# Row 1's overlap by transfers, the second dilated tile later, and the dilated v of rows 3 and 4 behind their transposes

## The chip, the cores and the metric

The kernel runs on one core of a Trainium2 chip, as one launch. The metric is device time in microseconds (us). Six runs of the kernel before gave 304.42 to 307.5, with a median of 305.58.

## The reference, cut to what matters

An attention over 8 batch rows, 8 heads, 576 tokens and 64 features feeds a two-layer network with a squared ReLU. Heads 0 to 3 see a sliding window of the last 32 tokens; heads 4 to 7 see every fourth of the last 128.

```python
B, H, S, D = 8, 8, 576, 64
rel = pos[:, None] - pos[None, :]
mask_plain = (rel >= 0) & (rel < 32)
mask_dil = (rel >= 0) & (rel < 128) & (rel % 4 == 0)
scores = where(mask of the head, q @ k.T / sqrt(D), -1e9)
attn = softmax(scores) @ v                    # per row and head
x = attn.transpose(0, 2, 1, 3).reshape(4608, 512)
h = x @ w_in                                  # 512 -> 2048
out = (maximum(h, 0) ** 2) @ w_out            # 2048 -> 512
```

## The kernel before, in words

**Two streams of work.** The attention goes by batch row (row 0 to row 7, 576 tokens each). The network goes by chunks of 512 tokens (chunk 0 to chunk 8). While row b's attention is computed, chunk b-1 of the network fills TensorE in between. The order of all instructions is written out by hand: each engine takes its instructions in the order in which the program records them, and waits for what it needs.

**Steps.** The network of a chunk is a generator (`moe_gen`), and `pump(n)` records n of its steps. In the first layer (`mm1_gen`) a step is two matmuls of a 128x512 tile `ph` (L305); two steps finish a tile, after which ScalarE takes the ReLU (`rt`, L328) and VectorE (DVE) the square (`g`, L329). So 32 steps make the first layer's 16 tiles. From chunk 2 on, the second layer (`mm2_strassen_gen`) is seven half-size products (L382) in place of eight; for that DVE forms sums of halves of g: `gs` (L338, L339), once after tile 11 and once, the last sums, after tile 15. TensorE reads them in the product named `pa<-wt,gs`, beginning with step 39; its fifth matmul is the first that needs the last sums. DVE then does a difference in g (L413) and one in gs (L425).

**The attention of a row.** `attn_scores` records four score groups, two sliding (`ps`, L588) and two dilated (`pz`, L613), each with a pump behind it. ScalarE takes the exponentials (`AT`, L572), DVE multiplies by the masks (`maskp`, `maskd`, L575). `attn_values` then records three sliding values tiles (`pav`, L643), and four dilated ones (`paw`, L659, for t = 0, 1 and a = 0, 1). DVE normalizes each (a reciprocal, L626, and a product into `xs` or `xd`, L631). The tiles pav and paw share two buffers in PSUM, so that each waits until the normalization of the tile two before is done. From row 4 on, `attn_values_by_dma` does the same, with the transposes of the result left to DMA.

**v and its overlap.** v is loaded in fp32 by SyncE's (SP's) DMA queue into `sv` (sliding) and `sd` (dilated), and GpSimd (POOL) casts it to fp16: `cast_sliding_v` makes three casts into `vp` (L169), `cast_dilated_v` four into `vd` (L177). Each sliding block of 96 queries needs 32 tokens of the block before it, and the second dilated tile (t = 1) needs 64 of the first. These are copied within vp and vd. `halo_sliding` and `halo_dilated` do it on ScalarE (L184: three copies a row, L189: two); `halo_sliding_by_dma` and `halo_dilated_by_dma` do it by one SP transfer each (L201, L204). Rows 0, 1 and 2 use ScalarE, rows 3 to 7 the transfers (from row 5 on, vp's copy is on DVE, L196).

**q and k of the next row.** POOL's DMA queue loads the sliding ones to `ns` (L112) and copies the dilated ones as fp16 to DRAM (`dd`, L214). DVE reorders ns into `nr` (`by_token`, L120), SP stores that (`dp`, L224), and SP transposes dp and dd into `QKTp` and `QKTd` (L232, L236). `turn` is the nr copy and the dp store. Before POOL loads the row after, it touches the last transposed tile (`seen`, L242), and so waits until that has landed.

**Where the next row's turn stands.** In rows 2 and 3 it is `turn_and_load`; row 2 records it behind the third pav, row 3 behind its second dilated score group. It records nr, dp, the loads of sv and sd, the four transposes, and all seven casts. From row 4 on, nr and dp stand behind the second (row 4) or third pav (rows 5 to 7), sd's load behind the transposes, and the dilated casts at the head of the next row, behind POOL's ns and dd.

The sums and the copy that the steps of the text follow:

```python
def sum_of_g(g, f0, f1):                      # DVE, L338 and L339
    k = slice(f0 - HF, f1 - HF)
    nc.vector.tensor_add(gs[0][:, k], g[:, k, HTOK:], g[:, f0:f1, HTOK:])
    nc.vector.tensor_sub(gs[1][:, k], gs[0][:, k], g[:, k, 0:HTOK])
```

Of the kernel before, what the change touches and what calls it, by code (L numbers as in the profile page):

```python
# [17 lines left out]
def kernel(  # L18
# [9 lines left out]
    nc = tc.nc  # L28
# [105 lines left out]
    def load_dilated_v(b, eng):  # L134
        vv = v[b, HH:H].rearrange("h (i c) d -> i h (c d)", c=DIL)
        for t in range(2):
            eng.dma_start(out=sd[P - QD[t] : P, t, :, :], in_=vv[Q0D[t] : Q0D[t] + QD[t]])
# [13 lines left out]
    def load_w_out(gs):  # L151
        for g in gs:
            nc.gpsimd.dma_start(
                out=wo[g],
                in_=moe_w_out[4 * g * P : 4 * (g + 1) * P, :].rearrange(
                    "(fl s) m -> fl (s m)", s=4
                ),
            )
# [8 lines left out]
    def cast_sliding_v(b, ms=range(0, NB, 2)):  # L167
        for m in ms:
            nc.gpsimd.tensor_copy(  # L169
                vp[b % 2][:, m : m + 2, :, 0:D], sv[:, :, m : m + 2, :].rearrange("p h m d -> p m h d")  # L170
            )

    def cast_dilated_v(b):
        for t in range(2):
            p0 = 64 * t
            for c in range(0, DIL, 2):
                nc.gpsimd.tensor_copy(  # L177
                    vd[b % 2][p0:P, t, c : c + 2, :, 0:D],
                    sd[p0:P, t, :, D * c : D * (c + 2)].rearrange("p h (c d) -> p c h d", d=D),
                )  # L180

    def halo_sliding(b, mp):
        m0, m1 = max(1, 2 * mp), 2 * mp + 2
        nc.scalar.copy(  # L184
            vp[b % 2][0:PADP, m0:m1, :, 0:D], vp[b % 2][P - PADP : P, m0 - 1 : m1 - 1, :, 0:D]
        )
# [13 lines left out]
    def halo_sliding_by_dma(b):  # L200
        nc.sync.dma_start(out=vp[b % 2][0:PADP, 1:NB], in_=vp[b % 2][P - PADP : P, 0 : NB - 1])  # L201

    def halo_dilated_by_dma(b):
        nc.sync.dma_start(out=vd[b % 2][0:64, 1], in_=vd[b % 2][64:P, 0])  # L204

    def cast_v(b):
        cast_sliding_v(b)
        cast_dilated_v(b)


    def keep_dilated_qk(b):
        d = dpool.tile([2, HH * CL, DIL * D], FP16, name=f"dd{b}", tag="dd")
        for i, src in ((1, k), (0, q)):
            nc.gpsimd.dma_start(  # L214
                out=d[i].rearrange("(r i) x -> r (i x)", i=4),
                in_=src[b, HH:H].rearrange("h (r i) d -> (h r) (i d)", i=16),
                max_dma_last_dim=4096,
            )
        return d
# [301 lines left out]
    def pump(n):  # L521
        for _ in range(n):
            while pending:
                try:
                    next(pending[0])
                    break
                except StopIteration:
                    pending.pop(0)
# [52 lines left out]
    def s_sliding(b, hp, between=None):  # L581
        tiles = [pa(f"ps{b}_{hp}_{half}") for half in range(2)]
        for half, ps in enumerate(tiles):
            for m3 in range(3):
                m = 3 * half + m3
                for e in range(2):
                    r = slice(D * e, D * (e + 1))
                    nc.tensor.matmul(  # L588
                        ps[:, e, QB * m3 : QB * (m3 + 1)],
                        QKTp[b % 2][r, 1, hp, QB * m : QB * m + P],  # L590
                        QKTp[b % 2][r, 0, hp, PADP + QB * m : PADP + QB * (m + 1)],
                        start=True,
                        stop=True,
                    )
        for half, ps in enumerate(tiles):
            exps(2 * hp + half, ps)
            if not between:
                masked(2 * hp + half, maskp)
        if between:
            between()  # L600
            for half in range(2):
                masked(2 * hp + half, maskp)
# [30 lines left out]
    def x_tiles(b):  # L633
        x = xp.tile([QB, 2, NB, 2, D], FP16, name=f"xs{b}", tag="xs")
        return x, [xp.tile([QD[t], DIL, HH, D], FP16, name=f"xd{b}_{t}", tag=f"xd{t}") for t in range(2)]
# [77 lines left out]
    def attn_scores(b, gap, less=0, hooks={}):  # L713
        for hp in range(2):
            s_sliding(b, hp)
            if hp in hooks:
                hooks[hp]()
            pump(gap)
        for g in range(2):
            s_dilated(b, g)  # L720
            if 2 + g in hooks:
                hooks[2 + g]()
            if g and b < 3:
                halo_sliding(b, 0)
            pump(gap - less)

    def attn_values(b, gap, wide=False, then=None):
        xs = x_tiles(b)
        for mp in range(3):
            av_sliding(b, mp, xs)  # L730
            if b < 3:
                if mp < 2:
                    halo_sliding(b, mp + 1)
                else:
                    halo_dilated(b, 0)
            if then and b == 2 and mp == 2:
                then()
            pump(gap)
        x_sliding(b, 0, xs, wide)
        if b < 3:  # L740
            halo_dilated(b, 2)
        pump(gap)
        av_dilated(b, 0, 0, xs)
        if then and b == 1:
            then()
        pump(gap)
        x_sliding(b, 1, xs, wide)
        pump(gap)
        av_dilated(b, 0, 1, xs)
        pump(gap)  # L750
        for a in range(2):
            av_dilated(b, 1, a, xs)
            pump(gap)
        x_dilated(b, 0, xs, wide)
        pump(gap)
        x_dilated(b, 1, xs, wide)

    def attn_values_by_dma(b, then):
        xs = x_tiles(b)
        for mp in range(3):  # L760
            av_sliding(b, mp, xs)
            if mp == (2 if b > 4 else 1):
                then[0]()
            pump(3)
        x_sliding_by_dma(b, xs)
        ys = []
        for t in range(2):
            for a in range(2):
                av_dilated(b, t, a, xs)
                pump(4 + 2 * (a > t))  # L770
            ys.append(x_dilated_by_dma(b, t, xs))
            then[1 + t](ys[t])
        pump(6)
        x_from(b, 0, ys[0])
        pump(7)
        x_from(b, 1, ys[1])
# [34 lines left out]
    nc.gpsimd.tensor_copy(sd[64:P, :, :, 0], wi[2][64:P, :, 0:2].rearrange("p d f -> p f d"))  # L811
    load_v(1)
    cast_sliding_v(1)
    load_w_out((3,))
    ns = load_sliding_qk(2)
    cast_dilated_v(1)
    dd = keep_dilated_qk(2)
    for mp in (1, 2):
        av_sliding(0, mp, xs)
# [42 lines left out]
    for b in range(2, 4):  # L862
        pending.append(moe_gen(b - 1))
        nxt = b + 1
        after_transposes(b)
        ns = load_sliding_qk(nxt)
        if b == 2:
            cast_v(b)
        dd = keep_dilated_qk(nxt)
        if b == 3:  # L870
            halo_sliding_by_dma(b)
            halo_dilated_by_dma(b)

        def turn_and_load():
            dp = turn(nxt, ns)
            load_sliding_v(nxt)
            load_dilated_v(nxt, nc.sync)
            transpose_sliding(nxt, dp)
            transpose_dilated(nxt, dd)
            cast_v(nxt)  # L880

        pump(22 if b == 2 else 12)
        attn_scores(b, 4, 0, {3: turn_and_load} if b == 3 else {})
        attn_values(b, b, False, turn_and_load)
        pump(1000)

    for b in range(4, B):
        pending.append(moe_gen(b - 1))
        nxt = b + 1
        if nxt < B:  # L890
            after_transposes(b)
            ns = load_sliding_qk(nxt)
            dd = keep_dilated_qk(nxt)
        if b > 4:
            cast_dilated_v(b)
        else:
            halo_sliding_by_dma(b)
        halo_dilated_by_dma(b)
        dps = []

        def copied():
            if nxt < B:
                dps.append(turn(nxt, ns))

        def first(y):
            if nxt < B:
                load_sliding_v(nxt)

        def second(y):
            if nxt < B:  # L910
                transpose_sliding(nxt, dps[0])
                transpose_dilated(nxt, dd)
                load_dilated_v(nxt, nc.sync)
                nc.gpsimd.tensor_copy(seen, y[:, 0, 0, 0:1])
                cast_sliding_v(nxt)
                at_end.append(lambda: halo_sliding_at_end(nxt))

        pump(3)
        attn_scores(b, 3)
        attn_values_by_dma(b, (copied, first, second))  # L920
        pump(1000)
    pending.append(moe_gen(B - 1))
# [32 lines left out]
```

## Time and profile before

| | us |
|---|---|
| median of six runs (lowest, highest) | 305.58 (304.42, 307.5) |
| profiled execution, its own time | 304.42 |
| its span, first to last instruction | 302.3 |
| busy: TensorE, DVE, ScalarE, POOL | 286.3, 209.7, 173.1, 62.0 |
| first ph matmul of chunk 2 (beside row 3) | 93.75 |
| of chunks 3, 4, 5, 6 (beside rows 4 to 7) | 125.38, 155.16, 185.95, 216.25 |

How to read it. PE is TensorE, PEld its weight loads, ACT ScalarE, and SPq SyncE's DMA queue. A row of the timeline has its start and duration in us, engine, line, operation, output<-inputs, shape and count; in brackets stands the idle time of the engine before it and what ended that. Operations on one engine overlap at their ends, so a g product of 0.42 recurs every 0.33 when they stand back to back, and two of them make 0.75. A row of the windows view has the window, its length, the busy time of PE, PEld, DVE, ACT and POOL with the number of their instructions, the granted clock, the DMA share and GB/s. A row of the waits has who waited for whom, the total in us, the times, and the longest.

### The profile page before, as it was taken

The page shows a single profiled execution, that of the slowest core. Times are in us where ns is not written, and L with a number is a line of the kernel's source. Part 1 is how long each engine was busy: PE and PEld are TensorE (multiplying, and loading weights), DVE is VectorE, ACT ScalarE, POOL GpSimd, SP SyncE. Part 2 cuts the span into 40 slices and gives each one's busy share as a digit, 9 for nine tenths or more (in the row PEclk, how much of TensorE's full clock was granted, in tenths as well). Part 3 has the DMA queues.
Part 4 walks back from the last instruction along what each step waited for, and adds up shares of the span by engine and source line. Part 5 has one row for each costly group of instructions (what it writes and reads, how often), then busy time and mean ns, then how long its engine had stood idle before and what let it go on. Part 6 is the DMA issues. An engine that isn't in the chain of part 4 may idle for free.

```text
span 302.3 us, 6890 instructions
## 1 busy us (share of the span) xinstructions
PE 286.3 (95%) x2760; PEld 192.0 (64%) x2760; DVE 209.7 (69%) x437; ACT 173.1 (57%) x293; POOL 62.0 (21%) x112
## 2 busy tenths in 40 slices
PE   1888998999999999999999999999999999999994
PEld 1454554555555468756889977568756975785583
DVE  7784448758852798489859984998499835734652
ACT  1856648568745953495358535953595356426620
POOL 4481009002605303320027002700230000000000
PEclk9999999999999999999999999999999999999999
DMA  6999997899599999996799999989983230003004
GB/s 113 195 198 214 206 182 133 184 211 229 128 212 183 240 205 179 247 201 124 129 182 256 191 133 191 265 179 164 179 230 41 41 139 0 2 4 136 3 0 139
DMA packets 77471, 46.77 MB, mean 155 GB/s; under 512 B 58432, under 2 KB 69184, under 8 KB 77440
## 3 DMA queue, kind: packets, MB, share of 16 engines
q1 hardware_dynamic: 68688, 32.71, 51.9%
q0 software_dynamic: 8752, 13.63, 26.4%
q8 instruction: 21, 0.34, 0.5%
q14 instruction: 10, 0.08, 0.1%
HBM read 36.70 MB, written 16.52 MB: 176 GB/s over the span
## 4 chain that ended last, share of the span: by engine, by line
PE 76%; DVE 7%; DMA 6%; ACT 4%; POOL 3%; issue 2%; DVEq 0%; POOLq 0%
PE ph L305 32%; PE pa L382 15%; PE po L450 9%; PE pb L382 8%; DMA vd<-vd 4%; PE pc L382 3%; DMA nd<-in_q_dram 2%; PE paw L659 2%; DVE g L329 2%; DVE xd L631 2%; PE ps L588 1%; ACT AT L572 1%; PE pav L643 1%; POOL ns L112 1%; DVE gs L338 1%
## 5 line engine op out<-in xcount | busy, mean ns | idle before, releaser
L305 PE MATMUL ph<-xT,wi 128*128 128x512 f16 (+1 forms) x640 | 134.2, 359 | 0.7 <-ACT xT L696 0.7
L328 ACT ACTIVATE rt<-ph 128x512 f16<-128x512 f32 x144 | 86.3, 609 | 44.5 <-PE ph L305 42.3
L305 PEld LDWEIGHTS <-wi 128*128 128x128 f16 x640 | 68.2, 114 | 45.8 <-issue 0.6
L329 DVE TENSOR_TENSOR g<-rt 128x512 f16<-128x512 f16 x144 | 63.1, 450 | 37.4 <-ACT rt L328 36.3
L382 PEld LDWEIGHTS <-g 128*128 128x128 f16 x448 | 43.3, 98 | 6.3 <-DVE g L329 0.2
L382 PEld LDWEIGHTS <-gs 128*128 128x128 f16 x336 | 32.0, 98 | 5.2 <-DVE gs L339 1.7
L450 PE MATMUL po<-wo,g 128*128 128x512 f16 x128 | 33.1, 379 | 0.0
L382 PE MATMUL pa<-wt,gs 128*128 128x256 f16 x224 | 27.6, 273 | 0.8 <-DVE gs L339 0.8
L409 DVE TENSOR_TENSOR ov<-pb,ov 128x512 f32<-128x512 f32 x14 | 9.7, 691 | 26.0 <-ACT ov L398 13.0
L382 PE MATMUL pb<-wt,g 128*128 128x256 f16 x224 | 27.1, 273 | 0.0
L398 ACT COPY ov<-pa 128x512 f32<-128x512 f32 x14 | 8.2, 585 | 31.0 <-PE pa L382 31.0
L169 POOL CAST vp<-sv 128x512 f16<-128x512 f32 x24 | 14.2, 626 | 53.1 <-DMA sv<-in_v_dram 49.2
L177 POOL CAST vd<-sd 128x512 f16<-128x512 f32 (+1 forms) x32 | 21.8, 708 | 10.9 <-DMA sd<-in_v_dram 8.1
L631 DVE TENSOR_TENSOR xd<-paw,rcp_d 80x512 f16<-80x512 f32 (+1 forms) x32 | 21.9, 684 | 1.1
L572 ACT ACTIVATE AT<-pz 128x576 f16<-128x576 f32 x32 | 19.8, 695 | 1.1 <-PE pz L613 1.1
L572 ACT ACTIVATE AT<-ps 128x576 f16<-128x576 f32 x32 | 19.2, 658 | 1.3 <-PE ps L588 0.8
L575 DVE TENSOR_TENSOR AT<-AT,maskd 128x576 f16<-128x576 f16 x32 | 17.6, 573 | 2.3 <-ACT AT L572 1.1
L575 DVE TENSOR_TENSOR AT<-AT,maskp 128x576 f16<-128x576 f16 x32 | 15.2, 484 | 4.8 <-ACT AT L572 3.0
L631 DVE TENSOR_TENSOR xs<-pav,rcp_p 96x512 f16<-96x512 f32 x24 | 16.5, 687 | 0.8
L398 ACT COPY ou<-pa 128x512 f32<-128x512 f32 x14 | 8.2, 585 | 13.9 <-PE pa L382 13.7
L450 PEld LDWEIGHTS <-g 128*128 128x128 f16 x128 | 10.4, 97 | 8.3
L659 PEld LDWEIGHTS <-AT 128*128 128x128 f16 x256 | 11.9, 98 | 5.6 <-PE paw L659 1.3
(81 smaller groups left out, 273.3 us busy)
## 6 DMA issues: line engine op xcount, KB each, us to landing
sv<-in_v_dram SPq DMA_DIRECT2D x14, 288.0 KB, 5.4
dp<-nr SPq DMA_DIRECT2D x12, 288.0 KB, 4.1
out_dram<-ou SPq DMA_DIRECT2D x6, 512.0 KB, 4.3
out_dram<-ov SPq DMA_DIRECT2D x6, 512.0 KB, 5.0
sd<-in_v_dram SPq DMA_DIRECT2D x8, 320.0 KB, 6.3
ns<-in_k_dram POOLq DMA_DIRECT2D x8, 288.0 KB, 6.7
ns<-in_q_dram POOLq DMA_DIRECT2D x8, 288.0 KB, 7.7
sd<-in_v_dram SPq DMA_DIRECT2D x8, 256.0 KB, 6.2
```

Of the source, the lines that this page charges most:

```text
L169: nc.gpsimd.tensor_copy(vp[b % 2][:, m : m + 2, :, 0:D], sv[:, :, m : m + 2, :].rearrange("p h m d -> p m h d"))
L177: nc.gpsimd.tensor_copy(vd[b % 2][p0:P, t, c : c + 2, :, 0:D], sd[p0:P, t, :, D * c : D * (c + 2)].rearrange("p h (c d) -> p c h d", d=D),)
L305: nc.tensor.matmul(ph[:, t0:t1], wi4[ffc // 4][:, dmk, :, ffc % 4], xT[:, dmk, x0 : x0 + t1 - t0], start=(dmk == 0 and t0 == 0), stop=(dmk ...
L328: nc.scalar.activation(rt, ph[:], ACTF.Relu)
L329: nc.vector.tensor_mul(g[:, ffc, :], rt, rt)
L382: nc.tensor.matmul(banks[bank][:, t], a(k, t), b(k), start=(new and t == 0 and k == 0), stop=(k == HF - 1), skip_group_check=True,)
L398: nc.scalar.copy(ot, banks[A])
L450: nc.tensor.matmul(po, g[:, ffc, t * P : (t + 1) * P], wo[ffc // 4][:, ffc % 4, :], start=(ffc == 0), stop=(ffc == NFF - 1),)
L572: nc.scalar.activation(AT[:, u, 0:UW], ps[:, :, 0 : UW // 2], ACTF.Exp, scale=scale)
L575: nc.vector.tensor_mul(AT[:, u, 0:UW], AT[:, u, 0:UW], mask)
L631: nc.vector.tensor_tensor(out=x, in0=pv, in1=rb, op=ALU.mult)
L659: nc.tensor.matmul(pav[:, e, h * (D + 2) : h * (D + 2) + D + 1], AT[:, 4 + h, off : off + P], vd[b % 2][:, t, 2 * a + e, h, 0 : D + 1], st ...
```

## The change

- **Row 1** takes the overlap of vp and vd by two SP transfers, recorded right behind the casts of each, in place of five ScalarE copies.
- **Rows 2 and 3** (`turn_and_load`): the load of sd stands behind the four transposes, and only the sliding casts remain there. The dilated casts of rows 3 and 4 move to the head of these rows, behind POOL's ns and dd and ahead of the vd transfer.
- **Row 3** records its scores after 9 steps and not 12, and its turn (nr and dp of row 4) behind the second pav in place of the second dilated score group.
- **Rows 4 to 7**: the second dilated tile (t = 0, a = 1) follows 7 steps behind the first in place of 4; 3 steps follow it in place of 6.

```diff
@@ attn_scores
-            if g and b < 3:
+            if g and b == 2:
                 halo_sliding(b, 0)
@@ attn_values
-            if b < 3:
+            if b == 2:
                 if mp < 2:
                     halo_sliding(b, mp + 1)
                 else:
                     halo_dilated(b, 0)
-            if then and b == 2 and mp == 2:
+            if then and b > 1 and mp == 4 - b:
                 then()
             pump(gap)
         x_sliding(b, 0, xs, wide)
-        if b < 3:
+        if b == 2:
             halo_dilated(b, 2)
@@ attn_values_by_dma
                 av_dilated(b, t, a, xs)
-                pump(4 + 2 * (a > t))
+                pump((7, 3)[a] if t == 0 else 4)
@@ before row 1
     cast_sliding_v(1)
+    halo_sliding_by_dma(1)
     load_w_out((3,))
     ns = load_sliding_qk(2)
     cast_dilated_v(1)
+    halo_dilated_by_dma(1)
     dd = keep_dilated_qk(2)
@@ rows 2 and 3
         dd = keep_dilated_qk(nxt)
         if b == 3:
+            cast_dilated_v(b)
             halo_sliding_by_dma(b)
             halo_dilated_by_dma(b)
 
         def turn_and_load():
             dp = turn(nxt, ns)
             load_sliding_v(nxt)
-            load_dilated_v(nxt, nc.sync)
             transpose_sliding(nxt, dp)
             transpose_dilated(nxt, dd)
-            cast_v(nxt)
-
-        pump(22 if b == 2 else 12)
-        attn_scores(b, 4, 0, {3: turn_and_load} if b == 3 else {})
+            load_dilated_v(nxt, nc.sync)
+            cast_sliding_v(nxt)
+
+        pump(22 if b == 2 else 9)
+        attn_scores(b, 4)
         attn_values(b, b, False, turn_and_load)
@@ rows 4 to 7
-        if b > 4:
-            cast_dilated_v(b)
-        else:
+        cast_dilated_v(b)
+        if b == 4:
             halo_sliding_by_dma(b)
         halo_dilated_by_dma(b)
```

## The prediction

> **What bounds the kernel now.** The page first: TensorE is busy nearly all of the span, at a granted clock of 0.9 or more in every slice. Only its gaps can be saved, so I looked next at TensorE's waits.
>
> ```profile
> PE 286.3 (95%) x2760; PEld 192.0 (64%) x2760; DVE 209.7 (69%) x437; ACT 173.1 (57%) x293; POOL 62.0 (21%) x112
> ```
>
> Behind the start (24.6 us, untouched) its waits are few. This view shows those that the change can meet:
>
> ```profile
> PE pa L382 <- DVE gs L339: 0.8, 2, 0.5
> PE pav L643 <- ACT vp L184: 0.5, 1, 0.5
> PE pav L643 <- DVE xs L631: 0.3, 1, 0.3
> ```
>
> In the timeline of TensorE they lie in row 1 (51 us), row 3 (111 us) and rows 5 and 6 (176 and 207 us):
>
> ```profile
> 51.37 0.29 PE L643 MATMUL pav<-vp,AT 128*128 128x65 f16 x4 [0.54 <-ACT vp L184]
> ...
> 111.33 0.42 PE L643 MATMUL pav<-vp,AT 128*128 128x65 f16 x8 [0.27 <-DVE xs L631]
> ...
> 207.07 1.49 PE L382 MATMUL pa<-wt,gs 128*128 128x256 f16 x12 [0.35 <-DVE gs L339]
> ```
>
> Row 4 has no such wait. I compared rows 4 and 6, from the first ph matmul to the first product with gs: the same DVE operations, but POOL casts vd inside row 6's window only.
>
> ```profile
> 125.38:145.56 20.18, 20.18 (x203) 12.18 (x202) 17.57 (x40) 13.95 (x25) 2.61 (x5) 1.00 0.86 187
> 185.95:206.12 20.17, 20.17 (x202) 12.19 (x201) 17.98 (x39) 13.95 (x25) 5.43 (x9) 1.00 0.99 219
> ```
>
> DVE's timeline shows what those casts do: the same two g products and two masks, row 4 and then row 6, with the casts between.
>
> ```profile
> 132.47 0.92 DVE L329 TENSOR_TENSOR g<-rt 128x512 f16<-128x512 f16 x2
> 133.51 1.00 DVE L575 TENSOR_TENSOR AT<-AT,maskd 128x576 f16<-128x576 f16 x2
> ...
> 145.17 0.69 DVE L339 TENSOR_TENSOR gs<-gs,g 128x1024 f16<-128x1024 f16 x1
> ```
>
> ```profile
> 192.29 2.94 POOL L177 CAST vd<-sd 128x512 f16<-128x512 f32 x4
> ```
>
> ```profile
> 193.17 1.58 DVE L329 TENSOR_TENSOR g<-rt 128x512 f16<-128x512 f16 x2
> 194.68 1.23 DVE L575 TENSOR_TENSOR AT<-AT,maskd 128x576 f16<-128x576 f16 x2
> ...
> 206.32 0.69 DVE L339 TENSOR_TENSOR gs<-gs,g 128x1024 f16<-128x1024 f16 x1
> ```
>
> Beside the casts two g products take 1.58 us, without 0.92. The last sums end at 145.87 (20.48 behind row 4's first ph) and at 207.01 (21.06 behind row 6's). TensorE wants them four matmuls of 0.11 into the product, at 20.61. So row 4 makes it by about 0.1 and row 6 waits. From 195.8 to 207 DVE has no gap: what is lost beside the casts comes out as a TensorE wait. DVE is what sets these rows.
>
> **Row 1: overlap by transfers.** Five copies leave ScalarE, 1.44 (three of vp) + 0.62 + 0.61 = 2.67 us. Is ScalarE the path there? TensorE waits 0.54 for the first, but what it feeds is DVE:
>
> ```profile
> 49.30 2.73 DVE L575 TENSOR_TENSOR AT<-AT,maskd 128x576 f16<-128x576 f16 x4
> 51.95 0.19 DVE L626 RECIPROCAL rcp_p<-pav 96x8 f32<-96x8 f32 x1
> ```
>
> DVE masks until 52.0 and takes up pav the moment it is done; pav is needed by 51.95, not by 50.95. The next pav at 53.01 needs the buffer that DVE frees at 52.87 (the view names a vd copy, which ends at the same moment). From there DVE runs on to 59.2 with one gap of 0.6, a round trip through TensorE. So 0. Bounds: a gain up to 0.7 (the wait and its neighbour, were DVE not behind it). The new transfers: SP issues vp's when its casts end, 46.46; such a transfer landed 3.0 to 3.7 after issue, so about 50.2, with cover until 51.6. vd's is issued after the second cast, 49.8; it landed in 2.2 to 7.4 (median 6.0), about 55.9, with cover until 57.1 (third paw). At 7.4 it costs 0.1 to 0.3. Behind both on SP's queue stands the dp store, whose data come at 56.7: nothing waits. ns2 beside them lands at 55.2 and is read at 56.0; 0.2 MB more at 206 GB/s would make that up to 0.3.
>
> **Row 2, SP's and POOL's queues.** Four transposes (5.16 + 2.79 of issue) now precede the two sd loads (3.13). QKTp comes up to 3.1 earlier and is wanted 3 steps of 0.43 = 1.3 earlier (the pump before row 3's scores falls from 12 to 9): covered, 0, with a loss up to 0.5 if it is late. The vd casts of row 3 move behind QKTd's landing, the two ns and two dd issues (2.4 us) and sd's landing: sd is issued from about 96 to 99 and takes 6.2 to 7.4. So they run at about 103 to 106, where DVE does row 3's masks and g products; now they run at 95.7 to 98.4, where DVE has slack. SP's vd transfer waits for them; behind it stands the dp4 store, not ready before 111. Nobody waits.
>
> **Row 3.** Attention starts 3 steps earlier, row 4's copy nr follows the second values tile. DVE runs from 106.40 to 114.06 without a gap that matters, 7.66 us, up to the last sums. Of this, two masks (0.73) now come before 106.40 and the third normalization (0.20 + 0.69, 0.84 dense) comes in: 7.77. The fourth score group (0.36 of TensorE) now precedes that g: start 106.76, end 114.53. The casts: six masks and products in row 6 took 3.82 (192.01 to 195.83); back to back they are 4 x 0.37 + 2 x 0.33 = 2.14; the difference is 1.7, some 1.5 of it beside the casts. Row 3 has gaps of 0.7 left between 103.5 and 106.4: net 0.8, end 115.34. TensorE resumes at the fifth gs matmul then; before it did at 114.19, with one paw group (0.26) still ahead that is now done. Loss 115.39 - 114.19 - 0.26 = **0.94**. Bounds: 0.1 without the casts, 1.6 with 1.5 in full. That the two waits of row 3 (0.44 and 0.17 over the pace) go is in this sum: what is late next is the sums.
>
> **Row 4.** Its four casts come from row 3's tail, 120.4, into its own window, as rows 5 and 6 have it. Those waited 0.64 and 0.51 more than row 4; mean **0.57**, bounds 0.3 (casts early, in gaps) and 0.75. The vd transfer waits for the casts (about 134) and lands some 6 later, wanted by the third paw at 143: covered. SP's dp5 store behind it has its data at 138.
>
> **Second dilated tile, rows 4 to 7.** The same DVE operations stand before the last sums; the tile's normalization changes places with one g product. TensorE reaches the tile 1.3 later, at about 202.4 in row 6, and DVE is not there before 204.3. So 0, bounds -0.1 and 0.1: rows 5 and 6 keep their waits.
>
> **A rule against the change.** Rows 4 and 6 price four casts at 0.6 net. The Trainium skill, "SBUF — State Buffer", section "Who interferes with whom", says that a DVE instruction with two SBUF inputs contends with a GpSimd one that reads SBUF, and that the loser blocks for the whole instruction. Read so, my estimate is four casts of 0.61 blocking 2.4, and rows 3 and 4 losing about 1 more each than above; the trace shows less, since POOL gives way too (0.74 a cast).
>
> **Sum.** 0.94 + 0.57 = 1.5. The profiled execution took 304.42 (span 302.3, 2.1 around it), which becomes 305.9. It was the fastest of the six, whose median is 305.58: 307.1.
>
> **Rivals.**
> *DVE as above*: 307.1, chance 0.64; alone it spans 306.0 to 308.3.
> *Faster: ScalarE's copies set row 1.* Over its pace (0.216 a 512-wide matmul, 0.027 a pav one) TensorE loses 2.1 in row 1 between 48.9 and 57.5. If the pav at 53.01 really waited for the vd copy, as the view says, and the rest follows from that, up to 2.1 goes: 305.0 with the loss of rows 3 and 4, 303.9 where their casts cost only 0.4. It decides at whether row 1's DVE rows close up behind 52.0. Against it: they have no gap to close but the 0.6. Chance 0.12.
> *No change: the casts find slack.* sd lands 3 earlier than I reckon (in rows 5 and 6 it took 4.2 to 5.2), before the masks: rows 3 and 4 lose 0.1 to 0.4 together, 305.9. Chance 0.12.
> *Much slower: a late transfer.* If row 1's vp transfer takes the worst 7.4, it lands at 54.0 instead of 51.6: 2.4 more, 309.5. Chance 0.12.
>
> **The numbers.** About 0.5% (1.5 us) is what a measurement of this kernel can tell from no change; it puts the borders at 304.05 and 307.1. The likeliest case splits 0.37 slower and 0.27 same; the late transfer adds 0.12 slower, the slack case 0.12 same, the ScalarE case 0.10 faster and 0.02 same. The range, 305.0 to 308.8, leaves out most of the ScalarE case and the worst of the late transfer, less than 0.2 together; within it lie the bounds of rows 1 to 4 (0.1 + 0.3 - 0.7 and 1.6 + 0.75 + 0.5, on 305.58).
>
> **What would show it.** Right: POOL's vd casts inside row 3's masks and row 4's, with g products of 0.8 beside them; the last sums over 20.61 behind the first ph in row 4; a wait before gs in rows 4, 5 and 6, and before the third pav and gs in row 3; in row 1 the same DVE rows without gaps. Wrong: row 1's DVE rows ending before 59, or no TensorE wait in row 4.

## The result and the profile after

The changed kernel takes 307.71 us (median of 17 runs, 306.27 to 310.08), the kernel before 306.24 in the runs beside it. The ratio is 1.0067 with a 95% interval of 1.0044 to 1.0089, which is 1.3 to 2.7 us slower. It is taken over fast executions alone, so it isn't the quotient of these two medians: four slow ones of the 38 before are left out. The forecast was 307.1, range 305.0 to 308.8. The profiled execution of the changed kernel took 310.84 (span 309.1) and is no typical one: a second profile (below) took 308.72. The page:

```profile
PE 288.7 (93%) x2760; PEld 193.9 (63%) x2760; DVE 213.0 (69%) x437; ACT 170.6 (55%) x288; POOL 65.5 (21%) x112
...
PEclk9999999699999999999999999999999999999999
```

TensorE's share falls from 95 to 93%, and in one slice, the eighth (54.1 to 61.8), the granted clock drops. The waits of TensorE that the change could meet:

```profile
PE pav L643 <- DMA vp<-vp: 5.0, 3, 3.1
PE pa L382 <- DVE gs L339: 0.9, 2, 0.5
```

The new one is not DVE's. Three times TensorE waits inside the first pav of a row for vp's overlap transfer (L201), 5.0 in all. The timeline of TensorE has them in rows 1, 3 and 4, and the old waits before gs in rows 5 and 6, which stay:

```profile
54.02 0.38 PE L643 MATMUL pav<-vp,AT 128*128 128x65 f16 x4 [3.12 <-DMA vp<-vp]
...
112.65 0.29 PE L643 MATMUL pav<-vp,AT 128*128 128x65 f16 x4 [1.20 <-DMA vp<-vp]
...
140.34 0.29 PE L643 MATMUL pav<-vp,AT 128*128 128x65 f16 x4 [0.63 <-DMA vp<-vp]
...
183.09 1.48 PE L382 MATMUL pa<-wt,gs 128*128 128x256 f16 x12 [0.48 <-DVE gs L339]
...
213.44 0.83 PE L382 MATMUL pa<-wt,gs 128*128 128x256 f16 x6 [0.41 <-DVE gs L339]
```

What L201 took from issue to landing, from the view of that line, first before (two transfers), then after (three):

```profile
DMA to landing us min/median/max: 3.0/3.3/3.7
```

```profile
DMA to landing us min/median/max: 5.4/6.6/7.9
```

What runs beside it is seen in row 3 on SP's and POOL's queues. The two sd loads now stand ahead of the transfer, land 5.3 after issue, and so run beside it. And since QKTd lands earlier, POOL's ns loads, which wait for it, go out 0.44 ahead of the transfer in place of 1.26 behind it. Before, from SP's and POOL's rows:

```profile
101.15 0.61 SPq L201 DMA_DIRECT2D vp<-vp  x1
```

```profile
102.41 0.65 POOL L112 DMA_DIRECT2D ns<-in_k_dram  x1 [0.38 <-DVE g L329]
```

After, the same two queues:

```profile
102.95 1.32 SPq L137 DMA_DIRECT2D sd<-in_v_dram  x2
104.38 1.53 SPq L473 DMA_DIRECT2D out_dram<-ot  x3
106.00 0.71 SPq L201 DMA_DIRECT2D vp<-vp  x1
```

```profile
105.56 0.65 POOL L112 DMA_DIRECT2D ns<-in_k_dram  x1
```

The chain of waits of the changed kernel from 100 to 113 (start, length, what) runs through the transfer and through no row of DVE:

```profile
106.00 6.61 DMA vp<-vp
112.61 0.04 issue
112.65 0.29 PE pav L643 x4
```

**Row 1 and the clock.** Windows of the changed kernel, whose columns are those of the prediction's windows:

```profile
52.00:54.00 2.00, 0.00 (x0) 0.00 (x0) 0.77 (x1) 0.00 (x0) 2.00 (x4) 0.72 1.10 225
54.00:56.00 2.00, 1.98 (x16) 1.14 (x16) 1.13 (x4) 0.00 (x0) 0.33 (x1) 0.50 1.20 216
...
58.00:60.00 2.00, 2.00 (x17) 1.09 (x15) 0.32 (x2) 0.64 (x1) 0.00 (x0) 0.57 0.78 144
60.00:62.00 2.00, 2.00 (x29) 1.19 (x27) 1.97 (x4) 1.03 (x2) 0.00 (x0) 1.00 0.00 0
```

Some 2 us into the wait the granted clock falls to 0.50 and stays there until 59.7. Row 1, from its first pav to the first ph of chunk 1, grows from 10.40 to 14.86: 2.6 by the longer wait (3.12 in place of 0.54) and 1.9 behind it, at half clock. Rows 3 (1.10), 4 (0.79) and 5 to 7 (0.26) add the remaining 2.2.

**Row 4.** Here are the windows of the changed kernel from the first ph to the first product with gs, row 4 and then row 6, as the prediction has them for the kernel before, and what DVE does beside the casts in row 4:

```profile
131.00:151.97 20.97, 20.34 (x203) 12.22 (x202) 18.59 (x40) 13.95 (x25) 5.40 (x9) 1.00 0.93 185
192.26:212.43 20.17, 20.17 (x202) 12.16 (x201) 17.97 (x39) 13.95 (x25) 5.51 (x9) 1.00 0.98 218
```

```profile
133.42 1.51 DVE L575 TENSOR_TENSOR AT<-AT,maskp 128x576 f16<-128x576 f16 x2 [0.30 <-ACT AT L572]
134.85 1.58 DVE L329 TENSOR_TENSOR g<-rt 128x512 f16<-128x512 f16 x2
```

The forecast's picture of the casts is there: masks of 1.51 in place of 1.00, two g products in 1.58 in place of 0.92. But row 4 is 0.8 longer already at the first product with gs, and waits for nothing there.

### The profile page after: what moved, and what is told of

The parts are those of the page before. It is cut to its first block, busy times and chain, and to the rows that moved or that the text cites. A ratio compares the mean times of both kernels' runs of the same rounds, so it can differ in the third digit from the quotient of the medians.

```text
span 309.1 us, 6882 instructions
## 1 busy us (share of the span) xinstructions
PE 288.7 (93%) x2760; PEld 193.9 (63%) x2760; DVE 213.0 (69%) x437; ACT 170.6 (55%) x288; POOL 65.5 (21%) x112
## 4 chain that ended last, share of the span: by engine, by line
PE 60%; DMA 27%; DVE 5%; POOL 2%; issue 2%; SPq 1%; ACT 1%; POOLq 0%; DVEq 0%
PE ph L305 24%; PE pa L382 14%; PE pb L382 7%; DMA sv<-in_v_dram 7%; DMA vp<-vp 6%; PE po L450 6%; DMA wi<-in_moe_w_in_dram 5%; DMA ns<-in_q_dram 5%; PE pc L382 3%; DMA QKTp<-dp 3%; DMA vd<-vd 2%; PE paw L659 2%; PE pav L643 1%; DVE g L329 1%; PE ps L588 1%
## 5 line engine op out<-in xcount | busy, mean ns | idle before, releaser
L450 PE MATMUL po<-wo,g 128*128 128x512 f16 x128 | 35.1, 396 | 0.0
L169 POOL CAST vp<-sv 128x512 f16<-128x512 f32 x24 | 15.5, 677 | 52.9 <-DMA sv<-in_v_dram 52.8
L177 POOL CAST vd<-sd 128x512 f16<-128x512 f32 (+1 forms) x32 | 23.1, 750 | 12.0 <-PE ph L305 8.0
L575 DVE TENSOR_TENSOR AT<-AT,maskd 128x576 f16<-128x576 f16 x32 | 19.9, 655 | 1.4 <-ACT AT L572 0.8
L575 DVE TENSOR_TENSOR AT<-AT,maskp 128x576 f16<-128x576 f16 x32 | 16.4, 531 | 5.1 <-ACT AT L572 4.0
L643 PEld LDWEIGHTS <-AT 128*128 128x128 f16 x192 | 9.8, 101 | 11.6 <-issue 6.7
L643 PE MATMUL pav<-vp,AT 128*128 128x65 f16 x192 | 11.1, 199 | 5.1 <-DMA vp<-vp 5.0
```

The source lines that it names most:

```text
L169: nc.gpsimd.tensor_copy(vp[b % 2][:, m : m + 2, :, 0:D], sv[:, :, m : m + 2, :].rearrange("p h m d -> p m h d"))
L177: nc.gpsimd.tensor_copy(vd[b % 2][p0:P, t, c : c + 2, :, 0:D], sd[p0:P, t, :, D * c : D * (c + 2)].rearrange("p h (c d) -> p c h d", d=D),)
L450: nc.tensor.matmul(po, g[:, ffc, t * P : (t + 1) * P], wo[ffc // 4][:, ffc % 4, :], start=(ffc == 0), stop=(ffc == NFF - 1),)
L575: nc.vector.tensor_mul(AT[:, u, 0:UW], AT[:, u, 0:UW], mask)
L643: nc.tensor.matmul(pav[:, i, h * (D + 2) : h * (D + 2) + D + 1], AT[:, 2 * (h // 2) + m // 3, off : off + P], vp[b % 2][:, m, h, 0 : D + 1 ...
```

## The experiments

Lengths in the profiled executions, in us. Row 1 is from its first pav to chunk 1's first ph; the others are from the first ph of the chunk beside the row to that of the next. Row 2 was 32.8 in all.

| kernel | ratio to before, 95% | row 1 | row 3 | row 4 | row 5 | row 6 | row 7 |
|---|---|---|---|---|---|---|---|
| before | | 10.40 | 31.63 | 29.78 | 30.79 | 30.30 | 29.78 |
| changed | 1.0067 (1.0044 to 1.0089) | 14.86 | 32.73 | 30.57 | 30.70 | 30.36 | 30.08 |
| changed, second profile (e10) | 1.005 (1.0014 to 1.0086) | 12.45 | 32.01 | 31.36 | 30.92 | 30.48 | 29.77 |
| e1 row 1 only | 1.0036 (1.0 to 1.0072) | 11.04 | 32.38 | 29.78 | 30.71 | 30.53 | 30.12 |
| e2 without row 1 | 1.0054 (1.0024 to 1.0084) | 10.55 | 32.00 | 31.52 | 30.72 | 30.41 | 30.67 |
| e3 sd early | 1.0108 (1.0073 to 1.0143) | 10.45 | 33.06 | 30.85 | 31.02 | 30.51 | 29.77 |
| e4 casts at head | 1.0048 (1.002 to 1.0076) | 10.17 | 32.71 | 29.77 | 30.74 | 30.57 | 29.87 |
| e5 tile only | 0.9975 (0.9948 to 1.0001) | 10.41 | 31.63 | 29.77 | 30.83 | 30.28 | 29.78 |
| e6 overlap on DVE | 1.0007 (0.9978 to 1.0036) | 10.73 | 32.64 | 29.77 | 30.52 | 30.49 | 29.78 |
| e7 early sd | 0.9933 (0.9902 to 0.9964) | 10.26 | 31.64 | 29.77 | 29.94 | 29.77 | 30.09 |
| e8 row 1's vd only | 0.9999 (0.9968 to 1.003) | 10.24 | 31.94 | 29.77 | 30.74 | 30.47 | 30.75 |
| e9 row 1 later | 1.0185 (1.0133 to 1.0236) | 15.69 | 31.64 | 29.77 | 30.67 | 30.47 | 30.10 |
| e11 cured | 0.9996 (0.9958 to 1.0035) | 10.41 | 36.73 | 29.77 | 29.94 | 29.77 | 29.78 |
| e12 early sd and the rest | 0.9965 (0.993 to 0.9999) | 12.02 | 32.60 | 30.38 | 29.94 | 29.78 | 30.15 |

One profile tells a row only so well. Where an edit did not reach, row 7 still went from 29.77 to 30.75 (e8) and row 3 to 32.38 (e1), each time with TensorE waiting 0.7 to 0.9 for QKTp before the row's first scores; and row 1, untouched in e12, took 12.02 there, with waits of 0.66 and 1.18 for DVE.

**e1: row 1 alone.** The kernel before with

```diff
     cast_sliding_v(1)
+    halo_sliding_by_dma(1)
...
     cast_dilated_v(1)
+    halo_dilated_by_dma(1)
```

and row 1's five ScalarE copies out. 

> The kernel before with row 1's overlap alone taken by the two SP transfers; rows 2 to 7 as before. By the forecast (DVE's dense chain sets row 1, both transfers land under cover) the ratio is 1.000 to 1.001 and the second half of the first pav starts no more than 0.6 later than the first half, as before. By the late-transfer rival the vp transfer takes over 4 us and lands behind 52, TensorE waits 1 to 3 us inside the first pav, and the ratio is 1.002 to 1.007; if that idle time reaches about 3 us the granted clock falls to 0.5 behind it, as in the profiled execution of the changed kernel, for about 1.9 more.

Measured: 1.0036. The transfer took 5.6, TensorE waited inside the first pav, and row 1 grew by 0.64 at full clock. So it is the late-transfer rival:

```profile
52.53 0.29 PE L643 MATMUL pav<-vp,AT 128*128 128x65 f16 x4 [1.43 <-DMA vp<-vp]
```

The clock did not fall in this execution. In 6 of the 11 executions that the ratio counts the mean clock was 0.994; those six have a median of 308.4, the five without 305.73, and the kernel before had 306.04 beside them. So the loss of this kernel lies mostly in the executions whose clock fell. How much of it is a longer wait and how much the clock, the times don't tell apart.

**e8: row 1's vd alone.** As e1, with vp's three copies kept on ScalarE and no vp transfer. 

> The kernel before with vd's overlap of row 1 alone by transfer; vp's three copies stay on ScalarE. The vd transfer has cover until the third paw, so if only the vp transfer makes row 1 longer, this run is at 1.000 (0.999 to 1.001) with row 1 at 10.4 from first pav to first ph. If ScalarE's vd copies held row 1 (the faster rival), up to 0.4 goes: 0.9985. If the vd transfer is late as well, row 1 gets longer by 0.3 or more.

Measured: 0.9999, row 1 at 10.24, the 0.54 before the first pav as before. The vd transfer landed 4.85 behind the first pav, under cover. So row 1 loses by vp's transfer and not by vd's. The faster rival (ScalarE's vd copies hold row 1) shows no gain: row 1 is 0.16 shorter, and in e2 to e7, which leave row 1 as it was, it took 10.17 to 10.73. The ratio's interval alone would allow the 0.9985 of that rival.

**e9: row 1's vp transfer later.** As e1, vp's transfer recorded behind vd's. 

> The kernel before with row 1's two transfers, but vp's stands behind vd's on SP's queue and so goes out some 3.5 us later than in the run with row 1 alone; TensorE should wait 4 to 5.5 us inside the first pav. If an idle time of over about 3 us takes TensorE's clock down, as the changed kernel's profile suggests (3.1 us of idle time, clock 0.5 in the rows from 54 to 59.4, 1.9 lost behind it; 1.4 us of idle time in the run with row 1 alone and clock 1.00), the clock falls in every run (mean 0.98 to 0.992) and row 1 takes 4 to 5 (the wait) plus 1.5 to 2.7 more than before: ratio 1.018 to 1.025. If that dip came from something else, the clock stays at 0.997 or more and the ratio is 1.012 to 1.016.

Measured: 1.0185, all four runs with a mean clock of 0.984 to 0.994. The timeline and the clock in the windows:

```profile
56.39 0.38 PE L643 MATMUL pav<-vp,AT 128*128 128x65 f16 x4 [5.06 <-DMA vp<-vp]
```

```profile
56.00:58.00 2.00, 1.61 (x15) 1.04 (x15) 0.89 (x2) 0.00 (x0) 0.00 (x0) 0.50 0.93 173
58.00:60.00 2.00, 2.00 (x21) 1.19 (x19) 1.46 (x4) 0.00 (x0) 0.00 (x0) 0.70 0.02 3
```

The wait brings the clock down, as the clock theory has it, but the price behind it was 0.8 in this execution (half clock for 3.4, mean 0.994), under the 1.5 to 2.7 expected. The other three, at 0.984 to 0.989, took 1.8 to 2.6 us longer and have no profile.

**e10: the changed kernel again.** No edit. 

> The changed kernel once more, for a second profile. The first one (310.84) took 3.1 more than the median of the changed kernel, and its row 1 was 4.4 longer than before. If the late transfer of row 1 varies with when sv lands, this profile shows a row 1 longer by 0.5 to 2, no dip of the clock, and rows 3 and 4 longer by 0.4 to 1.1 and 0.8 to 1.7, TensorE waiting for the vp transfer before their first pav.

Measured: 1.005. Row 1 grew by 2.05, row 3 by 0.38, row 4 by 1.58, the rest by 0.3; together 4.3, the difference of the two profiled times (308.72 and 304.42). In the expectation only "no dip of the clock" missed: here the clock fell after a wait of 1.73.

```profile
52.54 0.38 PE L643 MATMUL pav<-vp,AT 128*128 128x65 f16 x4 [1.73 <-DMA vp<-vp]
```

```profile
52.00:54.00 2.00, 1.46 (x14) 0.90 (x14) 1.13 (x3) 0.00 (x0) 0.66 (x2) 0.61 1.19 203
54.00:56.00 2.00, 2.00 (x16) 1.03 (x14) 1.32 (x4) 0.00 (x0) 0.00 (x0) 0.54 1.16 238
```

**e2: without row 1.** The changed kernel with row 1's copies on ScalarE. 

> The changed kernel with row 1's five copies back on ScalarE; everything else of the change kept. If the loss of the changed kernel (1.0067, about 2.0 us) is rows 3 and 4, this run keeps it: 1.005 by the forecast's sum (0.94 + 0.57), 1.006 by the chunk lengths of the changed kernel's profile (1.10 + 0.79). If it is row 1, this run is at 1.000 to 1.002.

Measured: 1.0054, so rows 3 and 4 carry most of the loss, as far as intervals that overlap can say so. Here row 4 waited longest, the transfer landing 8.8 after issue. In row 3 it took 6.8 and TensorE did not wait for it; the row's loss of 0.4 comes with a wait before gs, as forecast:

```profile
115.49 0.61 PE L382 MATMUL pa<-wt,gs 128*128 128x256 f16 x4 [0.62 <-DVE gs L339]
...
136.71 0.29 PE L643 MATMUL pav<-vp,AT 128*128 128x65 f16 x4 [1.58 <-DMA vp<-vp]
```

**e3: sd ahead of the transposes.** e2 with

```diff
             load_sliding_v(nxt)
+            load_dilated_v(nxt, nc.sync)
             transpose_sliding(nxt, dp)
             transpose_dilated(nxt, dd)
-            load_dilated_v(nxt, nc.sync)
```

> As the run without row 1's transfers, but rows 2 and 3 load sd ahead of the four transposes again; the dilated casts stay at the head of rows 3 and 4. By the forecast (casts beside the masks make DVE's sums late) nothing changes: ratio 1.005, last sums over 20.61 behind the first ph in row 4, waits before gs. By the rival that the changed profile suggests (the vp transfers of rows 3 and 4 are slow because sd's and ns's loads run beside them) the transfer is shorter, TensorE's waits before the first pav shrink from 1.20 and 0.63 to under 0.5 and 0.2, and the ratio falls to 1.001 to 1.003.

Measured: 1.0108, worse than either theory had it. The view of L201 bears out the rival: the transfers took 2.5 and 4.7, and no wait for them is left. But two things moved at once. sd no longer stands ahead of the transfer, and POOL's ns loads go out 1.0 and 1.6 behind it, where e2 had them 0.5 and 1.0 ahead.

```profile
DMA to landing us min/median/max: 2.5/3.6/4.7
```

The loss has another place. QKTd lands later now, POOL's touch of it (`seen`) holds ns, dd and the casts, and the casts start 10.2 (row 3) and 6.9 (row 4) behind the first ph, where e2 had them at 8.0 and 2.7. TensorE waits 2.0 before gs in the four rows 3 to 6, and 0.5 each for QKTp in rows 3 and 5. So both mechanisms exist, and the casts' price hangs on when they run.

**e4: the casts alone.** The kernel before with `cast_dilated_v` of rows 3 and 4 at the head of the row. 

> The kernel before with nothing changed but the four dilated casts of row 3 and of row 4, which move from the tail of the row before to the head of their own row, behind ns and dd; sd's load stays ahead of the transposes. By the forecast row 4 loses 0.57 and row 3 0.5 to 0.8 to DVE beside the casts: ratio 1.003 to 1.0045, TensorE waiting before gs. By the transfer theory the casts alone cost little: under 0.3, ratio 1.000 to 1.001.

Measured: 1.0048. Row 3 loses 1.08, row 4 nothing. POOL's rows of both, TensorE's wait in row 3, and row 4's window:

```profile
106.67 3.04 POOL L177 CAST vd<-sd 128x512 f16<-128x512 f32 x4
...
132.50 3.01 POOL L177 CAST vd<-sd 128x512 f16<-128x512 f32 x4
```

```profile
114.50 0.41 PE L643 MATMUL pav<-vp,AT 128*128 128x65 f16 x8 [1.24 <-DVE xs L631]
```

```profile
128.56:148.73 20.17, 20.17 (x203) 12.15 (x201) 18.45 (x40) 13.95 (x25) 5.49 (x9) 1.00 0.84 179
```

The casts take the same 3.0 in both. In row 3 they begin 10.8 behind the first ph, in row 4 only 3.95 behind it, ahead of DVE's dense stretch. DVE is busy 18.45 in that window against 17.57 before, and TensorE sees none of it.

**e6: vp's overlap of rows 3 and 4 on DVE.** e2 with `halo_sliding_at_end` behind the second score group (row 3) and at the end of row 3 (for row 4), no L201. 

> As the run without row 1's transfers, but vp's overlap in rows 3 and 4 is a DVE copy (about 0.49 each, the duration that L196 has in rows 5 to 7) in place of the SP transfer. If the late vp transfer makes rows 3 and 4 longer, its waits (1.6 in that run's profile) go and the chunks come back from 32.01 and 31.51 to under 31.9 and near 29.8 (the casts stand at 3 to 5 us into row 4, where they cost nothing in the run with the casts alone): ratio 1.001 to 1.003. If DVE's list is what sets them, as forecast, the added copies make both rows the same or longer: ratio 1.005 or more, with TensorE waiting before gs in row 4.

Measured: 1.0007. Row 4 is back at 29.77: its whole loss was the transfer. Row 3 stays at 32.64, with waits for DVE (0.66 before the third pav, 0.63 before gs): there DVE's list costs about as much as the transfer did in the changed kernel, but it has the added copy in it (0.79 in this row). In e2's row 3, with neither that copy nor a wait for the transfer, it cost 0.4.

**e5: the tile alone.** Only `pump((7, 3)[a] if t == 0 else 4)`. 

> The kernel before with the second dilated tile of rows 4 to 7 three steps later, nothing else. By the forecast 0 (bounds -0.1 and 0.1): rows 5 and 6 keep their waits before gs, the lengths of the chunks beside rows 4 to 7 stay at 29.78, 30.79, 30.30 and 29.78, ratio 1.000. Against it stands that row 7's chunk came out 0.3 and 0.9 longer in the two profiles that have the change of rows 3, 4 and the tile (but also 0.34 longer with row 1 alone): if the tile does it, the ratio is 1.001 to 1.003.

Measured: 0.9975, an interval that reaches to 1.0001, and rows 4 to 7 within 0.04 of before. The profile says 0.

**e7: the other direction.** The kernel before with

```diff
             dd = keep_dilated_qk(nxt)
+            load_dilated_v(nxt, nc.gpsimd)
-        if b > 4:
-            cast_dilated_v(b)
-        else:
+        if b == 4:
             halo_sliding_by_dma(b)
...
-                load_dilated_v(nxt, nc.sync)
                 nc.gpsimd.tensor_copy(seen, y[:, 0, 0, 0:1])
                 cast_sliding_v(nxt)
+                cast_dilated_v(nxt)
```

> The other direction, on the kernel before: for rows 5 to 7 sd is loaded on POOL's queue right behind dd, one row earlier, and the four dilated casts run at the end of the row before, behind the sliding ones, as rows 3 and 4 have them in the kernel before; no cast stands beside the masks of rows 5 to 7. If casts beside DVE's masks and g products cost rows 5 and 6 their waits before gs (0.64 and 0.51 over the pace), these go: 1.1 us faster, ratio 0.996 to 0.998, g products of 0.92 a pair, last sums under 20.61 behind the first ph. If the wait is from something else, the ratio is 0.999 to 1.002.

Measured: 0.9933, faster than both kernels. Rows 5 and 6 lose their waits before gs (30.79 and 30.30 become 29.94 and 29.77), and the g products stand at 0.92 a pair again:

```profile
186.15:206.32 20.17, 20.17 (x203) 12.14 (x201) 17.57 (x40) 13.95 (x25) 5.62 (x10) 1.00 1.04 216
```

Against row 6 of before DVE is busy 17.57 and not 17.98. The two rows gain 1.4 in the profile; that lies inside the interval of the ratio (1.1 to 3.0).

**e11: the change with both cures.** e2 with e7's load and casts for rows 3 to 7. 

> The changed kernel without row 1's transfers and with sd's load of rows 3 to 7 on POOL's queue right behind dd, the dilated casts at the end of the row before; the rest of the change (row 3's earlier scores, the turn behind the second pav, the later tile, vp's overlap by transfer) is kept. If the two causes found are all there is (sd's load beside the vp transfers of rows 3 and 4, and casts beside DVE's masks), the vp transfers take 2.5 to 5 us, row 3's chunk is 31.6 to 31.8, row 4's 29.8, rows 5 and 6 29.8 to 30.0: ratio 0.992 to 0.997, like the run with the early sd of rows 5 to 7. If row 3's earlier scores or the later turn cost by themselves, row 3 or 4 stays 0.4 or more longer.

Measured: 0.9996, not the 0.992 to 0.997 expected. The lengths of rows 4 to 7 are as expected. Row 4's transfer is not: it took 6.7, though sd no longer went out on SP's queue. POOL's ns loads went out 0.66 ahead of it, sd 1.67 behind it on POOL's queue, and it landed just in time. From SP's and POOL's rows, and the view of L201:

```profile
131.95 0.59 SPq L201 DMA_DIRECT2D vp<-vp  x1
```

```profile
131.29 0.63 POOL L112 DMA_DIRECT2D ns<-in_k_dram  x1 [0.36 <-issue]
```

```profile
DMA to landing us min/median/max: 2.5/4.6/6.7
```

Row 3 is 5.1 longer in this profile, whose execution took 308.36 against a median of 306.35: POOL's sd load now runs in row 2 beside sv's, the first transpose of QKTp took 6.5 to issue behind them, and TensorE waited for it and then ran at half clock. A load moved off one transfer landed on another:

```profile
100.88 0.54 PE L588 MATMUL ps<-QKTp 64*128 64x96 f16 x12 [3.03 <-DMA QKTp<-dp]
```

**e12: e7 and the parts not charged.** e7 with the later tile and row 3's turn behind the second pav, pump 12 kept. 

> The run with the early sd of rows 5 to 7, and on it the two parts of the change that no run has charged with a loss: the second dilated tile three steps later, and row 3's turn (nr and dp of row 4, and what follows them) behind the second pav; row 3's scores stay after 12 steps, its casts and row 4's at the end of the row before, sd ahead of the transposes. If these parts cost nothing, row 3's chunk is 31.5 to 31.7, those of rows 4 to 7 29.8 to 30.1, and the ratio 0.991 to 0.996 as without them. If the later turn by itself makes row 3 or row 4 late (its transposes land about 3 later), one of the two is 0.4 or more longer and the ratio 0.995 to 0.998.

Measured: 0.9965, in its profile rows 3 and 4 longer by 1.0 and 0.6. In row 3 0.9 of it is a wait for QKTp ahead of anything that the edit moved, in row 4 0.4 is a wait before gs. Whether the later turn costs by itself stays open.

## Why the prediction was right in its number and wrong in its place

- **The sum.** +1.5 was forecast; the ratio says 1.3 to 2.7. The sign, the range and the rank of the cases (slower, then same) hold. Of the terms, row 3's held in size, row 4's came about for another reason, row 1's was missed. That the sum came out is in part luck: most of the loss is a wait for vp's transfers, to which the sum gave nothing.
- **Row 1: 0 forecast, about 1 measured (e1: 0 to 2.2).** The step that failed is "such a transfer landed 3.0 to 3.7 after issue, so about 50.2". That was read from rows 3 and 4, where POOL's loads go out over 1 us behind it. In row 1 the last wo load goes out just ahead of it (in e9 long ahead) and the two ns loads beside it: 5.4, 5.6, 5.6 and 5.9 in four profiles. The forecast knew these loads (it counted what the transfer would do to ns2) and not what they do to the transfer. The late-transfer rival had the mechanism, with 2.4 for a landing in 7.4; what it lacked was that vp's casts themselves end 2.1 to 4.1 ahead of the first pav from execution to execution, and the clock. "DVE's dense chain sets row 1" held only as long as vp was there: in the changed kernel's first profile DVE has gaps of 1.67 and 1.70.
- **SP's queue: "Nobody waits".** Wrong, and in rows 3 and 4 it is the main cause. The step followed vd's transfer and the dp store past sd's load. It did not follow vp's transfer of rows 3 and 4, which keeps its place and its issue (1.40 behind row 4's first ph, 1.41 before) but has sd's load and the earlier ns beside it: 6.6 to 8.8, not 3.0 to 3.7. e2, e3 and e6 show from three sides that the late transfer makes the wait. Which load makes it late, no run tests alone. Over all profiles, the 19 transfers that went out ahead of POOL's ns took 2.5 to 5.0, and the 11 with a wo or ns load ahead of them 5.4 to 8.8. Of these 11, six had sd ahead as well (6.6 to 8.8), five had not (row 1's four, and e11's row 4: 5.4 to 6.7). So the transfer was late without sd ahead of it too; sd's own share is open. QKTp earlier and row 2 at 0 were right.
- **Row 3: 0.94 forecast, 0.4 to 1.1 measured.** The casts ran where they were put (from 108.42, which is 10.15 behind the first ph; forecast 9.3). Taken alone they cost 1.08 (e4). Without the transfer the row still lost 1.01, with a copy added to DVE's list (e6), and where the transfer came in time it lost 0.4 by the forecast's wait before gs (e2). In the changed kernel itself TensorE waits for the transfer (1.20 and 0.71 in its two profiles) and no longer for DVE, so that the two causes don't add.
- **Row 4: 0.57 forecast, 0.8 and 1.6 measured, none of it by the casts.** The step that the four casts come "into its own window, as rows 5 and 6 have it" failed: row 4's QKTd lands at its first ph, 3 to 4 earlier than theirs, so the casts start 2.7 to 4.0 behind it and not 6.3 to 6.8. There they cost 0 (e4, e6), below the lower bound of 0.3; at 6.9 they cost about 1 (e3). So the sign of a wait before gs in row 4 failed too.
- **Rows 5 and 6: casts beside DVE set their waits.** Right; e7 took the casts away and the waits went. It gives 0.85 and 0.53 for the two rows, where the forecast had 0.64 and 0.51.
- **Second tile: 0.** Right (e5).
- **What would show it.** Seen: the casts inside the masks of rows 3 and 4, the waits before gs in rows 5 and 6, row 4's last sums at 21.28. Not seen: a wait before gs in row 4 (the late sums follow a row that was late already), waits before the third pav and gs in row 3 (they are in e3 and e6, the one before gs in e2 too), row 1's DVE rows without gaps. The two signs of being wrong did not come either: TensorE did wait in row 4, but for the transfer, and row 1's DVE rows ended behind 59, but since they waited for TensorE. They could not tell this case from the forecast.
- **The rule against the change.** Read strictly, rows 3 and 4 would have lost 1 more each than forecast. With the casts alone (e4) row 3 lost 1.08 and row 4 nothing, though DVE was 0.9 busier there. In these runs the price went with the slack that DVE had at that moment.

## What to carry to other kernels

A small transfer's landing time hangs on its neighbours in flight (here 2.5 to 8.8 us for the same copy): before moving a load, list every small transfer with a short cover that will now run beside it, the ones that the edit doesn't touch too. The price of work beside a busy engine is set by when it starts within the row; take it from a row where it starts at the same moment. And a wait of TensorE of 2 us can cost more than itself.

## What the runs showed of the hardware that was not expected

The granted clock goes to half after rather short waits, and stays there for 3.4 us or twice that: 52.9 to 59.7 in the changed kernel (6.8 us), 52.4 to 55.9 in its second profile, 55.8 to 59.2 in e9, 101.1 to 104.5 in e11 (3.4 each), worked out from the clock in windows of 1 us. The waits were 3.12, 1.73, 5.06 and 3.03, and the clock fell 2.0, 1.6, 4.5 and 3.2 after TensorE's last matmul; e1's wait of 1.43 brought none. Half clock for 3.4 or 6.8 of some 306 us makes a mean of 0.994 or 0.989, at which many whole executions stand. Of 40 executions with row 1's transfers as in the change (the changed kernel and e1) 16 had one of 0.994 or less, of 101 of the kernel before 7. The Trainium skill, "TensorE: Matmul & The Clock Gate", Part 1, says that the clock is halved after an idle window of about 3.4 us. The length agrees with 3.4; that the whole window must be idle doesn't, since 1.6 was enough.

The loads of sd for rows 3 to 7 took 4.1 to 7.4 on SP's queue (the kernel before and the changed one) and 8.6 to 11.0 on POOL's (e7 and e11), there behind the loads of ns and dd or of dd alone. The issue of one transpose on SP grew to 6.5 us while loads ahead of it were in flight (e11); in the kernel before the longest was 4.1.
